# The last rows of a gated unit's weights: twelve rows a partition in the large load, eight small loads of equal rows on engines' own partitions

## The chip, the core and the metric

The kernel runs on one core of a Trainium2 chip. A core has engines with instruction streams of their own: PE (TensorE, matmuls), DVE (VectorE), ACT (ScalarE), POOL (GpSimd) and SP (SyncE, which here issues nearly all transfers). Sixteen DMA engines move data between HBM and SBUF, the on-chip memory of 128 partitions. The metric is the device time of one execution in microseconds (us), the median of several; here it was 199.22 us (three runs, 198.98 to 199.27). A change of less than about 0.2% can't be told from none.

## What is computed

One step of decoding for a batch of 8: a layer norm of x, attention over the last 2,048 entries of a key and value cache, and beside it a gated unit whose result scales the attention's output.

```python
W = min(4096, max(256, Sk // 4))                  # 2048
q = (xn @ wq).reshape(B, Sq, Hq, Dh)              # 8 x 1 x 32 x 128
scores = einsum("bhqd,bhkd->bhqk", q, k) * Dh ** -0.5   # k, v: the last W of the cache, 8 heads
o = einsum("bhqk,bhkd->bhqd", softmax(scores), v)
s = o.reshape(B, Sq, Hq * Dh) @ wo                # 4096 -> 512

g = einsum("bsd,df->bsf", xn, w_gate)             # D = 512, F = 1792
u = einsum("bsd,df->bsf", xn, w_up)
h = sigmoid(g) * u
d = einsum("bsf,fd->bsd", h, w_down)              # w_down: 1792 x 512
return x + s * silu(d)
```

All inputs are bf16. The change concerns w_down and the transposed h that is multiplied with it.

## The kernel before

The order of the work is written out by hand. All large inputs are loaded by SP on one queue, in the order in which the requests stand in the list `todo` (`want_rows`, `want_down`, `want_side`, `want_cache`): w_gate and w_up in two loads each, w_down, the two halves of wq, then 16 tiles of keys and 16 of values (2 MB each, 128 partitions x 16,384 bytes), the values three tiles behind, and wo in four pieces (16, 10, 4 and 2 of its 32 rows a partition). A tile needs one of nine slots (`empty`, L85); a request whose slot isn't free waits, and all behind it (`pump`, L87). SP also waits, for each load, for the one eight places earlier: there are eight completion semaphores for these loads.

A load over 128 partitions is spread evenly over the sixteen DMA engines, eight rows to each. A load over fewer partitions uses fewer engines.

The 1,792 rows of w_down are split. `want_down` (L143) loads the first 11 x 128 = 1,408 rows, 11 consecutive rows to a partition, so that a partition's piece is 11,264 bytes. The other 384 go into the tile `side` by eight small loads (`want_side`, L122; the list `sides`, L174):

- four of 15 rows a partition, over 5, 5, 3 and 3 partitions (`LOW`, `SF`): partitions q, q + 4, q + 8, ..., of the first 20, q being 0 to 3;
- four of 4 rows a partition, over 9 partitions each (`MID`, `SM`): partitions 32 + q, 32 + q + 4, and so on up to 67.

`side` must hold zeros where nothing is loaded in its first 32 partitions, so POOL clears them first (L126) and SP's first small load waits for that. Two small loads stand before the first half of wq in the queue, three before the second, three behind it.

PE multiplies xn with w_gate and w_up (L278, L294), ACT and DVE make h, and h is turned into columns: 11 transposes for the large part, 15 for the side part (L328), the latter from `h_side`, in which POOL has put the columns of h in the order of the side's partitions (L312, L320). DVE and ACT copy the result to `hT_sb` (L331, L333). Then 26 matmuls with 128, 68 or 20 rows make d (`d_ps`, L366), before the first transposes of keys (L456).

After that the loop over the batch runs: transposes of keys on PE with copies on DVE (L456, L461), scores (L474), softmax (L487 to L556), values (L584). It ends with the output projection `fin_ps` (L706), which takes wo's rows in the order in which they land, two operations on DVE (L717, L719) and the write of the output (L721).

Of the kernel before, what the change touches and what calls it, by code (L numbers as in the profile page):

```python
# [10 lines left out]
def kernel(  # L11
# [13 lines left out]
    nc = tc.nc  # L25
    P = 128
    B, _, D = A_x.shape
# [4 lines left out]
    F = B_w_gate.shape[1]  # L32
# [15 lines left out]
    bf16 = mybir.dt.bfloat16  # L48
# [12 lines left out]
    work = ctx.enter_context(tc.tile_pool(name="work", bufs=1))  # L61
# [20 lines left out]
    weights = {}  # L82
# [25 lines left out]

        todo.append((True, f))

    LOW, SF = (5, 5, 3, 3), 15
    MID, SM = 9, 4
    SP = 4 * max(LOW)
    M_AT = 32
    MP = 4 * MID
    MT = 11
    m0 = MT * P
    m1 = m0 + SF * sum(LOW)
    assert m1 + SM * MP == F
    side = {}  # L120

    def want_side(w, q, at, count, rows, base, of):  # L122
        def f(tag=None):
            if tag:
                t = slots.tile([P, SF, w.shape[1]], bf16, name="side", tag=tag)
                nc.gpsimd.memzero(t[:M_AT])  # L126
                side["t"] = t
                rows_of[("side", 0)] = (t, tag)
                for r in range(SF):
                    weights[("wd_sb", MT + r)] = t[: M_AT + MP if r < SM else SP, r]  # L130
            q0.dma_start(  # L131
                out=side["t"][at + q : at + q + 4 * (count - 1) + 1 : 4, :rows].rearrange(
                    "p s n -> p (s n)"
                ),
                in_=w[base : base + of * count * rows, :].rearrange(
                    "(p q s) n -> q p (s n)", q=of, s=rows
                )[q % of],
            )

        todo.append((not side, f))  # L140
        side["asked"] = True

    def want_down(w):  # L143
        def f(tag):
            t = slots.tile([P, MT, w.shape[1]], bf16, name="wd_sb", tag=tag)
            q0.dma_start(
                out=t[:].rearrange("p t n -> p (t n)"),
                in_=w[: MT * P, :].rearrange("(p t) n -> p (t n)", t=MT),
            )
            rows_of[("wd_sb", 0)] = (t, tag)  # L150
            for r in range(MT):
                weights[("wd_sb", r)] = t[:, r, :]

        todo.append((True, f))
# [16 lines left out]
    want_rows("wg_sb", B_w_gate, KT, 0, KT, 2)  # L171
    want_rows("wu_sb", B_w_up, KT, 0, KT, 2)
    want_down(B_w_down)
    sides = []  # L174
    for q in range(4):
        sides.append((q, 0, LOW[q], SF, m0 + q // 2 * 2 * LOW[0] * SF, 2))
        sides.append((q, M_AT, MID, SM, m1, 4))
    for x in sides[:2]:
        want_side(B_w_down, *x)
    for i in range(2):  # L180
        want_rows("wq_sb", A_wq, KT, 2 * i, 2 * i + 2)
        for x in sides[2 + 3 * i : 5 + 3 * i]:
            want_side(B_w_down, *x)
# [7 lines left out]
    for t0, t1 in ((0, 16), (16, 26), (26, 30), (30, RT)):  # L191
# [15 lines left out]
        out=perm[:].rearrange("k (l p) -> k l p", l=G),  # L207
        in_=ident[:].rearrange("k (p l) -> k l p", l=G),
# [11 lines left out]
        out=rstd[:], in_=mv[:, 1:2], func=AF.Sqrt, bias=eps_t[:], scale=1.0  # L220
# [4 lines left out]
        out=xn_bf[:],  # L225
# [8 lines left out]
    for kt in range(KT):  # L234
        nc.tensor.transpose(  # L235
            out=xnT_ps[:, kt, :],
            in_=xn_bf[:].rearrange("b (p kt) -> b kt p", kt=KT)[:, kt, :],
# [5 lines left out]

    hT_sb = work.tile([P, MT + SF, Z], bf16, name="hT_sb")
    nc.gpsimd.memzero(hT_sb[:])  # L245
    oP_sb = work.tile([P, RT, Z], bf16, name="oP_sb")
    nc.gpsimd.memzero(oP_sb[:])
    h_side = work.tile([B, SF, M_AT + MP], bf16, name="h_side")
    nc.gpsimd.memzero(h_side[:])

    NB = D // P
# [11 lines left out]
    with nc.allow_low_precision(reason="zeros and a one"):  # L263
        nc.vector.reduce_sum(
            out=band[:], in_=ident[:].rearrange("k (q t) -> k q t", t=RT), axis=AX.X
        )
        nc.vector.reduce_sum(
            out=pick[:], in_=ident[:].rearrange("k (q t) -> k t q", t=RT), axis=AX.X
# [21 lines left out]
    h_bf = ktpool.tile([P, CU * P], bf16, name="h_bf", tag="kT")  # L290
    for k in range(F // FC):
        u_ps = ps_t.tile([B, FC], f32, name="u_ps", tag="t")
        for kt in range(KT):
# [8 lines left out]
            out=h_bf[:B, k * FC : (k + 1) * FC],  # L302
# [5 lines left out]
    hT_ps = ps_m.tile([P, MT + SF, B], bf16, name="hT_ps", tag="m")  # L308
    for h in range(2):
        c = LOW[2 * h]  # L310
        at = m0 + h * 2 * LOW[0] * SF
        nc.gpsimd.tensor_copy(  # L312
            out=h_side[:, :, : 4 * c].rearrange("b t (e q) -> b t e q", q=4)[
                :, :, :, 2 * h : 2 * h + 2
            ],
            in_=h_bf[:B, at : at + 2 * c * SF].rearrange(
                "b (e q t) -> b t e q", q=2, t=SF
            ),
        )
    nc.gpsimd.tensor_copy(  # L320
        out=h_side[:, :SM, M_AT:],
        in_=h_bf[:B, m1:F].rearrange("b (p t) -> b t p", t=SM),
    )
    cuts = [h_bf[:B, :m0].rearrange("b (p t) -> b t p", t=MT)[:, t] for t in range(MT)]
    rows = [P] * MT + [M_AT + MP] * SM + [SP] * (SF - SM)
    cuts += [h_side[:, t, : rows[MT + t]] for t in range(SF)]
    for t, x in enumerate(cuts):
        nc.tensor.transpose(  # L328
            out=hT_ps[: rows[t], t, :], in_=x, identity=ident[:B, :B]
        )  # L330
    nc.vector.tensor_copy(out=hT_sb[:, :MT, :B], in_=hT_ps[:, :MT])  # L331
    for k, t0, t1 in ((M_AT + MP, MT, MT + SM), (SP, MT + SM, MT + SF)):
        nc.scalar.copy(out=hT_sb[:k, t0:t1, :B], in_=hT_ps[:k, t0:t1])  # L333

    def fold(out_ps, src, start, stop):
        for j in range(NB):
# [38 lines left out]
    for e in range(2):  # L375
# [3 lines left out]
        for r in range(rep):  # L379
            nc.tensor.transpose(  # L380
                out=qT_ps[:, r].rearrange("p g z -> p (g z)"),
                in_=q_bf[:, r * Dh : (r + 1) * Dh],
# [3 lines left out]
            out=qm_sb[:, :, G * e : G * (e + 1), M0 : M0 + rep].rearrange(  # L386
                "p b g r -> p r g b"
            ),
            in_=qT_ps[:, :, :, :B],
# [14 lines left out]
    for j in range(NB):  # L404
# [15 lines left out]
        out=turn_rows[:].rearrange("k (x l r) -> k x l r", x=NU, l=G),  # L420
        in_=ident[:].rearrange("k (l x r) -> k x l r", x=NU, l=G),
    )
    sel_e = consts.tile([P, 2, Hq], f32, name="sel_e")
    for e in range(2):
        nc.vector.reduce_sum(
            out=sel_e[:, e, :].rearrange("k (i h) -> k i h", i=NQ),
            in_=ident_f[:].rearrange(
                "k (i m e h) -> k e i h m", i=NQ, m=NJ // 2, e=2
            )[:, e],
# [290 lines left out]
    for j in range(NB):  # L720
        (q0, q1)[j % 2].dma_start(  # L721
            out=out.flatten_outer_dims()[:, j * P : (j + 1) * P],
            in_=y_bf[Z * j : Z * j + B, :],
# [31 lines left out]
```

## Time and profile before

| what | value |
|---|---|
| time, median of three runs | 199.22 us |
| the profiled execution: time, span of instructions | 199.33 us, 197.5 us |
| busy: PE, DVE, ACT, POOL | 80%, 63%, 21%, 6% of the span |
| moved by DMA | 81.32 MB in 6,396 packets, mean 412 GB/s |
| DMA, GB/s from 40 to 160 us | 429 |
| the issue of one small load on SP | 690 to 864 ns |
| POOL's clearing of `side`, 32 partitions x 3,840 words | 3,287 ns |

The trace also keeps a record of each DMA packet: one row of a load is one packet here. Durations in this execution:

```
bytes    packets   duration, ns
 2,048     128      84
 4,096     164     159
 7,168     512     272 in 465 cases, up to 1,412 in the first microsecond
10,240     128     385
11,264     128     422
15,360      16     573
16,384   4,480     611 in 4,437 cases, up to 1,159
16,384      16     879 to 962 (instructions, queue q8)
```

Share of busy time is an average; what matters for an edit is which wait ends last where it acts. In the profile's chain of waits, a DMA entry is the time from the issue of a load until the work that waited for it could start.

### The profile page before, as it was taken

To read this page: it belongs to the slowest core of one execution; us is meant where nothing else is said; L and a number is where in the kernel's file an instruction comes from. 1 tells how busy PE (TensorE), PEld (TensorE's weight loads), DVE (VectorE), ACT (ScalarE), POOL (GpSimd) and SP (SyncE) were. 2 spreads that over 40 slices of the span, in tenths; PEclk is the share of its full clock that TensorE was granted. 3 is DMA by queue.
4 is the path that set the end of the run, shared out by engine and by line. 5 is a ranking of instruction groups with operands and counts; after the bars stand their busy time and mean duration, and the time that the engine had idled before them with its cause. 6 is when DMAs were issued, how large, how long until landed. Compare 5 with 4: busy or idle time off the path is not lost.

```text
span 197.5 us, 4796 instructions
## 1 busy us (share of the span) xinstructions
PE 157.4 (80%) x2112; PEld 103.1 (52%) x2112; DVE 125.4 (63%) x245; ACT 40.7 (21%) x95; POOL 11.0 (6%) x22
## 2 busy tenths in 40 slices
PE   0089559999788898799979987999799979976733
PEld 0034325776664565466545654566466556655531
DVE  4623106999797696679666965796669658935201
ACT  0522022006306001600160016001600160071000
POOL 8910200000000000000000000000000000000000
PEclk9999859999999999999999999999999999999975
DMA  6999999999999999999999999999999999999980
GB/s 205 424 440 435 431 434 435 425 425 431 423 425 425 438 428 435 431 425 428 422 433 431 435 425 433 428 418 428 428 438 431 428 428 431 428 423 425 428 366 21
DMA packets 6396, 81.32 MB, mean 412 GB/s; under 512 B 812, under 2 KB 820, under 8 KB 1624
## 3 DMA queue, kind: packets, MB, share of 16 engines
q1 hardware_dynamic: 6328, 81.01, 96.6%
q8 instruction: 16, 0.26, 0.5%
q10 hardware_dynamic: 48, 0.01, 0.0%
q14 instruction: 4, 0.03, 0.0%
HBM read 81.01 MB, written 0.01 MB: 410 GB/s over the span
## 4 chain that ended last, share of the span: by engine, by line
DMA 73%; PE 22%; POOL 3%; SPq 0%; issue 0%; DVE 0%; POOLq 0%
DMA v_sb<-in_A_v_cache_dram 46%; DMA wo_sb<-in_A_wo_dram 14%; PE kT_ps L456 11%; DMA wq_sb<-in_A_wq_dram 7%; DMA k_sb<-in_A_k_cache_dram 6%; PE o_ps L584 4%; PE s_ps L474 3%; POOL side L126 2%; PE m_ps L614 1%; PE fin_ps L706 1%; PE pT_ps L563 1%; SPq L131 0%; POOL perm L206 0%; POOL hT_sb L245 0%; DVE prod L717 0%
## 5 line engine op out<-in xcount | busy, mean ns | idle before, releaser
L461 DVE COPY kT_sb<-kT_ps 128x1024 bf16<-128x1024 bf16 x128 | 84.2, 683 | 28.9 <-PE kT_ps L456 25.0
L456 PE MATMUL kT_ps<-perm,k_sb 128*128 128x128 bf16 x1024 | 72.6, 220 | 3.7 <-DMA k_sb<-in_A_k_cache_dram 3.7
L456 PEld LDWEIGHTS <-k_sb 128*128 128x128 bf16 x1024 | 58.8, 98 | 26.1 <-issue 16.8
L584 PE MATMUL o_ps<-v_sb,pT_sb 128*32 128x256 bf16 (+1 forms) x352 | 36.5, 327 | 9.0 <-DMA v_sb<-in_A_v_cache_dram 7.6
L474 PE MATMUL s_ps<-kT_sb,qm_sb 128*32 128x512 bf16 x256 | 25.6, 389 | 1.3 <-DVE kT_sb L461 1.1
L494 ACT ACTIVATE p_buf<-s_ps,st 32x512 bf16<-32x512 f32 x32 | 21.7, 679 | 15.4 <-DVE st L487 15.1
L584 PEld LDWEIGHTS <-pT_sb 128*32 128x32 bf16 (+1 forms) x352 | 12.3, 101 | 21.7 <-issue 19.7
L604 ACT ACTIVATE o_sb<-o_ps,fac 128x512 f32<-128x512 f32 (+1 forms) x8 | 4.9, 608 | 60.9 <-PE o_ps L584 60.9
L568 DVE COPY pT_sb<-pT_ps 128x1024 bf16<-128x1024 bf16 x16 | 10.8, 676 | 1.8 <-PE pT_ps L563 1.8
L474 PEld LDWEIGHTS <-qm_sb 128*32 128x32 bf16 x256 | 7.0, 93 | 8.0 <-issue 1.3
L563 PE MATMUL pT_ps<-turn_rows,p_buf 128*128 128x128 bf16 x128 | 10.7, 227 | 0.0
L563 PEld LDWEIGHTS <-p_buf 128*128 128x128 bf16 x128 | 9.4, 149 | 0.2 <-issue 0.2
L521 ACT ACTIVATE w_row<-w 1x128 f32<-1x128 f32 x8 | 2.5, 309 | 30.6 <-DVE w L514 30.6
L235 PE MATMUL xnT_ps<-ident,xn_bf 8*128 8x8 bf16 x4 | 0.3, 176 | 10.6 <-DVE xn_bf L224 10.6
L385 DVE COPY qm_sb<-qT_ps 128x128 bf16<-128x128 bf16 x2 | 1.4, 881 | 8.7 <-PE qT_ps L380 8.7
L301 DVE TENSOR_TENSOR h_bf<-sig,u_ps 8x448 bf16<-8x448 f32 x4 | 2.4, 608 | 6.6 <-PE u_ps L294 6.1
L278 PE MATMUL g_ps<-wg_sb,xnT_sb 128*8 128x448 bf16 x16 | 5.7, 544 | 0.3 <-DVE xnT_sb L242 0.3
L494 ACT ACTIVATION_READ_ACCUMULATOR p_buf<-s_ps,st 32x1 f32 x32 | 5.9, 184 | 0.0
L706 PE MATMUL fin_ps<-wo_sb,oP_sb 128*32 128x128 bf16 x128 | 3.3, 263 | 3.1 <-DMA wo_sb<-in_A_wo_dram 3.1
L487 DVE TENSOR_REDUCE st<-s_ps 128x1 f32<-128x512 f32 x8 | 5.4, 681 | 0.5 <-PE s_ps L474 0.5
L235 PEld LDWEIGHTS <-xn_bf 8*128 8x128 bf16 x4 | 0.2, 117 | 10.6 <-DVE xn_bf L224 10.6
L352 PE MATMUL q_ps<-wq_sb,xnT_sb 128*32 128x512 bf16 x32 | 3.1, 526 | 3.2 <-DMA wq_sb<-in_A_wq_dram 3.2
(88 smaller groups left out, 92.0 us busy)
## 6 DMA issues: line engine op xcount, KB each, us to landing
k_sb<-in_A_k_cache_dram SPq DMA_DIRECT2D x16, 2048.0 KB
v_sb<-in_A_v_cache_dram SPq DMA_DIRECT2D x16, 2048.0 KB
wq_sb<-in_A_wq_dram SPq DMA_DIRECT2D x2, 2048.0 KB
wo_sb<-in_A_wo_dram SPq DMA_DIRECT2D x1, 2048.0 KB
wg_sb<-in_B_w_gate_dram SPq DMA_DIRECT2D x2, 896.0 KB
wu_sb<-in_B_w_up_dram SPq DMA_DIRECT2D x2, 896.0 KB
wd_sb<-in_B_w_down_dram SPq DMA_DIRECT2D x1, 1408.0 KB
wo_sb<-in_A_wo_dram SPq DMA_DIRECT2D x1, 1280.0 KB
```

The lines of the kernel that those rows point to most:

```text
L126: nc.gpsimd.memzero(t[:M_AT])
L278: nc.tensor.matmul(g_ps[:], lhsT=xnT_sb[:, kt, :B], rhs=weights[("wg_sb", kt)][:, k * FC : (k + 1) * FC], start=(kt == 0), stop=(kt == KT ...
L456: nc.tensor.transpose(out=kT_ps[:, c, :], in_=k_sb[:, j * CU + h * CH + c, :], identity=perm[:],)
L461: nc.vector.tensor_copy(out=kT[(b, u)][:, h * CH : (h + 1) * CH, :], in_=kT_ps[:])
L474: nc.tensor.matmul(s_ps[b][NR * l : NR * (l + 1), :], lhsT=qm_sb[:, b, i * G + l, o : o + Z], rhs=t[:, :, PG * l : PG * (l + 1)], start=(u ...
L487: nc.vector.tensor_reduce(out=st[b][:], in_=s_ps[b][:], axis=AX.X, op=ALU.max, negate=True)
L494: nc.scalar.activation(out=p_buf[b % 2][rows, :, l, :], in_=s[rows, :].rearrange("k (c p) -> k p c", p=PG), func=AF.Exp, bias=st[b][rows, ...
L563: nc.tensor.transpose(out=pT_ps[:, c, :], in_=p_buf[b % 2][:, :, :, h * CH + c].rearrange("k p l -> k (p l)"), identity=turn_rows[:],)
L568: nc.vector.tensor_copy(out=pT[b][:, h * CH : (h + 1) * CH, :], in_=pT_ps[:])
L584: nc.tensor.matmul(o_ps[r] if b < WIDE else o_ps[r, 0:2], lhsT=pT[b][:, c, r], rhs=x, start=(c == 0), stop=(c == CU - 1), tile_position=(0 ...
L604: nc.scalar.activation(out=o[:, :n], in_=o_ps[:, :n], func=AF.Copy, scale=fac.pop(b)[:])
L706: nc.tensor.matmul(fin_ps[Z * j : Z * (j + 1), :], lhsT=oP_sb[:, t, :], rhs=weights[("wo_sb", t)][:, j * P : (j + 1) * P], start=(t == 0), ...
```

## The change

The large load takes 12 rows a partition (1,536 rows) instead of 11. The small loads bring the last 256 rows: 16 rows a partition, in two halves of 8 (8,192 bytes each), over 5, 5, 3 and 3 partitions. Their partitions lie 8 apart instead of 4 (`EP = P // 16`): a small load of pair h and parity q fills partitions p, p + 8, p + 16, ... with p = 2 (2h + q), that is 0, 2, 4 or 6. The loads over nine partitions are gone; the number of small loads, eight, and their places in the queue stay. POOL clears 40 partitions of `side` over 16 rows. `h_side` has 40 columns, of which every second stays zero; one of POOL's three copies and one of ACT's two go. There are 28 transposes and matmuls for d, 12 with 128 rows and 16 with 40.

```diff
-    LOW, SF = (5, 5, 3, 3), 15
-    MID, SM = 9, 4
-    SP = 4 * max(LOW)
-    M_AT = 32
-    MP = 4 * MID
-    MT = 11
+    LOW, SF = (5, 5, 3, 3), 16
+    EP = P // 16
+    SP = EP * max(LOW)
+    MT = 12
     m0 = MT * P
-    m1 = m0 + SF * sum(LOW)
-    assert m1 + SM * MP == F
+    assert m0 + SF * sum(LOW) == F

-    def want_side(w, q, at, count, rows, base, of):
+    def want_side(w, h, q, a, z):
         def f(tag=None):
             if tag:
                 t = slots.tile([P, SF, w.shape[1]], bf16, name="side", tag=tag)
-                nc.gpsimd.memzero(t[:M_AT])
+                nc.gpsimd.memzero(t[:SP])
...
+            n = LOW[2 * h]
+            at = m0 + 2 * h * LOW[0] * SF
+            p = 2 * (2 * h + q)
             q0.dma_start(
-                out=side["t"][at + q : at + q + 4 * (count - 1) + 1 : 4, :rows].rearrange(
-                    "p s n -> p (s n)"
-                ),
-                in_=w[base : base + of * count * rows, :].rearrange(
-                    "(p q s) n -> q p (s n)", q=of, s=rows
-                )[q % of],
+                out=side["t"][p : p + EP * (n - 1) + 1 : EP, a:z],
+                in_=w[at : at + 2 * n * SF, :].rearrange(
+                    "(p q s) n -> q p s n", q=2, s=SF
+                )[q, :, a:z],
             )
...
-    for q in range(4):
-        sides.append((q, 0, LOW[q], SF, m0 + q // 2 * 2 * LOW[0] * SF, 2))
-        sides.append((q, M_AT, MID, SM, m1, 4))
+    sides = [
+        (h, q, a, a + SF // 2)
+        for h in range(2)
+        for q in range(2)
+        for a in (0, SF // 2)
+    ]
...
-    nc.gpsimd.tensor_copy(
-        out=h_side[:, :SM, M_AT:],
-        in_=h_bf[:B, m1:F].rearrange("b (p t) -> b t p", t=SM),
-    )
...
-    rows = [P] * MT + [M_AT + MP] * SM + [SP] * (SF - SM)
-    cuts += [h_side[:, t, : rows[MT + t]] for t in range(SF)]
+    cuts += [h_side[:, t] for t in range(SF)]
+    rows = [P] * MT + [SP] * SF
...
-    for k, t0, t1 in ((M_AT + MP, MT, MT + SM), (SP, MT + SM, MT + SF)):
-        nc.scalar.copy(out=hT_sb[:k, t0:t1, :B], in_=hT_ps[:k, t0:t1])
+    nc.scalar.copy(out=hT_sb[:SP, MT:, :B], in_=hT_ps[:SP, MT:])
```

## The prediction, made before the change was run

> **What bounds the kernel now.** I read the page's slices first, then its queues, the chain of waits, SyncE's own timeline, and last the trace's record of every DMA packet (start, duration, bytes, queue).
>
> ```profile
> DMA  6999999999999999999999999999999999999980
> GB/s 205 424 440 435 431 434 435 425 425 431 423 425 425 438 428 435 431 425 428 422 433 431 435 425 433 428 418 428 428 438 431 428 428 431 428 423 425 428 366 21
> q1 hardware_dynamic: 6328, 81.01, 96.6%
> q8 instruction: 16, 0.26, 0.5%
> ```
>
> From the second slice to the last but two the sixteen DMA engines are never below nine tenths. The kernel moves 81 MB and is as long as that takes. PE, busiest of the others, is at 80%.
>
> ```profile
> 1.84 3.23 POOL side L126
> ...
> 6.81 13.68 DMA wq_sb<-in_A_wq_dram
> ...
> 163.50 28.32 DMA wo_sb<-in_A_wo_dram
> 191.86 1.86 PE fin_ps L706 x52
> 193.74 0.43 PE fin_ps L706 x8
> 194.19 0.30 DVE prod L717
> ```
>
> The chain (start, length, what) ends with the output weights landing: PE starts its last 8 matmuls at 193.74, when the last load is in, and the rest is fixed work (197.5 of span, 199.33 of time; that execution lies 0.11 above the median of 199.22). So the question is when the last engine has finished its last packet.
>
> ```profile
> 5.09 1.68 SPq L131 DMA_DIRECT2D side<-in_B_w_down_dram  x2
> 6.81 0.46 SPq L101 DMA_DIRECT2D wq_sb<-in_A_wq_dram  x1
> ...
> 20.51 2.58 SPq L159 DMA_DIRECT2D k_sb<-in_A_k_cache_dram  x4
> ...
> 57.01 0.53 SPq L159 DMA_DIRECT2D v_sb<-in_A_v_cache_dram  x1
> ```
>
> SyncE (first column the start) issues far ahead. The load issued at 57.01 is the thirteenth cache load; twelve such loads before it occupy even the quickest engine until 83. The cover is 26 us there and, worked out in the same way for the other loads, never under 14 from 26.73 on, so no engine runs dry.
>
> The packet records say who is last. On one engine packets follow each other end to start (4 ns overlap), so each engine's stream can be followed through its completion writes. A 16,384-byte packet takes 611 ns in 4,437 of 4,480 cases, 607 from start to start: 27 GB/s, sixteen times that is 432. The engines differ only in two things: the small side loads and the instruction packets. Row k of a small load goes to engine k: three streams hold four packets of 15,360 bytes, two hold two, four more hold only the 4,096s, seven none. Each 16,384-byte instruction packet (queue q8) delays the stream of its engine by some 1.42 us; they go round two of engines 5-8 and six of 9-15, twice. Two streams with equal phase were told apart by that order. Four smaller ones (q14) cost engines 0-4 another 0.55 to 0.85 each. Last completion, in us of the span (packet clock less 11.34):
>
> ```
> engines   small loads now          last completion
> 0-2       4 x 15360 + 4 x 4096     192.86  192.90  193.45
> 3-4       2 x 15360 + 4 x 4096     192.10  193.27
> 5-8       4 x 4096                 190.34  190.96  192.12  193.60
> 9-15      none                     189.99  192.86  192.92  193.02  193.14  193.18  193.25
> ```
>
> The last is one of 5-8 with two instruction packets: 193.60, and PE's 193.74 follows.
>
> **The change by bytes.** Same 81 MB, same 51 loads.
> - Large load L146: 12,288 bytes a row for 11,264. Between 422 ns (11,264) and 611 (16,384) lies 460: 8 rows x 38 ns = +0.30 us on every engine.
> - Small loads: 8,192 bytes lie at 310 ns between 272 (7,168) and 385 (10,240). Engines 0-2 had 4 x 573 + 4 x 159 = 2.93 us and get 8 x 310 = 2.48: -0.45, net -0.15. Engines 3-4: 1.78 to 1.24, net -0.24. Engines 5-8 lose 4 x 159 and four completion writes, -0.64, net -0.34. Engines 9-15 net +0.30.
> - The end by this: 193.60 - 0.34 = 193.26 on the old last engine, 193.25 + 0.30 = 193.55 on the new one. Sum -0.05 us.
>
> **Edits costed at nothing.** POOL's memset L126 (3.29 us for 3,840 words a row) gets 4,096: +0.22, and SyncE's first L131, wq_sb and all behind move with it. The chain counts this memset, but its cover is the queue: wg, wu and wd keep the engines busy to 14.6, while wq_sb is issued at 6.81. Without cover it would cost 0.22. The other memsets are +0.03 and -0.19. One of three POOL copies (L320, 0.30) and one of two ACT copies (L333) go; two transposes and two d_ps matmuls (some 0.11 each at L366) come. These lie before the first kT at 32.49, behind those 14 us of cover; without it they cost about 0.2. The chain of eight loads in flight keeps its numbering: k_sb still waits for the first wq_sb.
>
> **The change by place.** A small load's rows now lie 8 partitions apart (row k at 8k + 0, 2, 4 or 6) instead of 4 (4k + q, and 32 + 4k + q). Do these writes cross another engine's? In the large loads no engine ever stretches another, and the old small packets, 573 ns sixteen times and 159 each time, neither were stretched nor stretched a neighbour. Had engine k owned partitions 8k to 8k+7, nearly all old small packets would have crossed (engine 1's to 4-7, the 4,096s at 32-63). So either crossing costs nothing or the groups are 4 partitions wide with a second set 32 further on, which the old places fit for all nine engines. In that second case the new places cross: engine 1 writes to 8-11 (engine 2's) and 12-15 (3's), 2 to 16-19 (4's) and 20-23 (5's), 3 to 24-27 (6's), 4 to 32-35 (0's), 0 at last to 4-7 (1's).
>
> The trace of before holds no crossing, so its price is bounded. Low: nothing; the six 1,024-byte packets of x_bf overlapped in partitions 0-7 at 44 ns each, though so little may be held in buffers. High: an instruction packet of 16,384 bytes, which shares an engine instead, costs its stream 1.42 us, 8,192 bytes by that 0.71. Between, if two streams halve one path: 0.303 to each per packet. I take 0.303, the fair share; the fetch also has a latency that data in a queue doesn't.
>
> Each of engines 0-4 crosses or shares with four packets at the least: +1.21. On 0-2, that gives 193.45 - 0.15 + 1.21 = 194.51 for the latest, +0.91. Engine 3 crosses with four and is hit by four of engine 1's: +2.42, so 192.10 - 0.24 + 2.42 = 194.28, or, if it is the other of its pair, 195.45 (+1.85). If only the one that is hit loses, the end is +0.6 to +0.9. I take +1.1: 199.22 + 1.1 = 200.3 (the profiled execution 200.4). At 0.71 for four packets: 193.45 - 0.15 + 2.84 = 196.14, +2.5, 201.8.
>
> The Trainium skill speaks against this change in the same place. SBUF — State Buffer, section "Door 1: The DMA port swizzle", says that four neighbouring partitions and the four 32 further on share one write port of 27.2 GB/s, not eight neighbours. DMA: Bandwidth & Descriptors, section "The descriptor swizzle", gives one engine to one port in 128-row loads, on this chip's hardware queues too. By these, the old places are each engine's own and the new ones are not, and two streams on one port halve: an estimate of 8,192 / 27.2 = 0.30 us a packet, the same sum. The unstretched packets of before agree with it; no run so far shows a crossing.
>
> **Rivals.**
> - *Crossing is free (0.27).* Then only bytes count: 199.22 - 0.05 = 199.17, not slower. For it: x_bf's overlapping packets, and the small loads are only 256 KB, some of which may wait in buffers. Against: sixteen engines keep 432 GB/s only in loads where the rows fit the groups. It decides if engines 0-3 end by 193.6.
> - *Eight neighbours are one engine's own, as the change has it, and something was lost before (0.08).* The old last engine then shows its full -0.34: 198.88. Against: 9-15 get +0.30 whatever else happens and stood at 193.25, so it needs start phases that favour them by 0.3 (the engines' ends of wd spread from 14.56 to 15.28 here).
> - *Crossing at the fetch's price, or engines 1 and 2 hit as often as they hit (0.15, within the slower side).* Price +2.5: 201.8. Against: while one engine writes elsewhere its own path is free, so the five small loads partly pass each other.
> - *The rest, 0.50, is the forecast*, +0.6 to +1.85.
>
> **How the numbers follow.** The likeliest is 200.3, its own range 199.8 to 201.1. The first rival lies at 199.17 with a spread of 0.15 between executions, so the range reaches from 199.0 to 201.6: it leaves out half of the 0.08 and more than half of the 0.15. About 0.2% (0.4 us) is what a measurement can tell from no change. Slower by more: 0.50 + 0.15, less 0.04 for a small price within 0.4 us, 0.61. Within: 0.27 + 0.04, and part of the second rival, 0.32. Faster by more: 0.07.
>
> **What would show it.** Right: small packets of 8,192 bytes above 310 ns (up to 600), 16,384-byte packets near 900 to 1,200 in the stretch from 14 to 32 us on engines 3, 5 and 6 besides those beside instruction packets, GB/s in that stretch below 430, and the last completion on one of engines 0-4. Wrong: 8,192 bytes at 310 ns throughout and the last completion on one of 9-15 near 193.55. The sum by bytes fails if 12,288 bytes take other than 460 ns, or if an engine idles between loads.

## The result and the profile after

The changed kernel takes 201.05 us (median of four, 200.86 to 201.41) against 199.20: 1.0098 times as long, interval 1.0083 to 1.0113. It is slower, by 1.85 us. Its profiled execution has a span of 199.5 us (197.5 before) and a time of 201.41 (199.33).

The slices of the changed kernel's page, and its queues:

```profile
DMA  6999999999999999999999999999999999999980
GB/s 214 420 447 406 373 340 437 427 437 424 419 440 427 427 420 437 434 434 420 427 434 422 443 420 430 432 424 437 417 430 434 430 437 417 424 435 430 423 354 19
q1 hardware_dynamic: 6288, 81.01, 96.6%
q8 instruction: 16, 0.26, 0.5%
```

The same megabytes pass through engines that count as just as busy. But in the fourth, fifth and sixth slice (a slice is 5 us; these reach from 15 to 30 us) they move 406, 373 and 340 GB/s, where the kernel before moved 435, 431 and 434. An engine whose packet takes longer is as busy as before, so the DMA digits show nothing; the row of GB/s shows it. These slices are where the small loads run.

The end of its chain of waits (start, length, what):

```profile
165.36 28.52 DMA wo_sb<-in_A_wo_dram
193.88 0.04 issue
193.92 1.26 PE fin_ps L702 x30
...
195.82 0.43 PE fin_ps L702 x8
...
196.27 0.30 DVE prod L713
```

The same last steps as before, 2.08 us later (prod at 196.27 for 194.19). Nothing was lost behind the loads.

SP's timeline in the changed kernel:

```profile
5.31 1.62 SPq L131 DMA_DIRECT2D side<-in_B_w_down_dram  x2
6.98 0.43 SPq L101 DMA_DIRECT2D wq_sb<-in_A_wq_dram  x1
...
21.56 2.58 SPq L157 DMA_DIRECT2D k_sb<-in_A_k_cache_dram  x4
...
59.53 0.54 SPq L157 DMA_DIRECT2D v_sb<-in_A_v_cache_dram  x1
```

The first small load is issued 0.22 later, as the longer memset has it, and this vanishes: wq_sb follows 0.17 later than before and the engines are still busy with w_down then. The keys are issued 1.05 later, because they wait for the first half of wq, which lands later; they are still issued before the second half of wq has been moved.

The packet records show where the time went. (The packet clock's offset to the span differs from execution to execution; from here on it is taken from each profile's own first instruction, which lies at 0.24.) The durations in the changed kernel:

```
12,288 bytes   128 packets    460 ns in 126 cases
 8,192 bytes    32 packets    309 ns in 14 cases, 18 longer, up to 642
16,384 bytes    in three stretches at the small loads (14 to 32 us) 92 longer than 620,
                up to 1,313; elsewhere only beside instruction packets
```

The lengthening in the three stretches, summed and divided by the sixteen engines, is 0.31, 0.71 and 0.90 us: 1.93 for an engine on the mean. It isn't the loss of a few of them: the streams that can be followed from end to end lost 1.86 to 1.91, and one that holds no small load goes 611, 908, 616 in the first stretch, 825, 1,033, 685 in the second and 1,086, 1,029 in the third.

### The profile page after: what moved, and what is told of

Its sections match the earlier page's. It is cut to its first block, busy times and chain, and to the rows that moved or that the text cites. A ratio compares the mean times of both kernels' runs of the same rounds, so it can differ in the third digit from the quotient of the medians.

```text
span 199.5 us, 4801 instructions
## 1 busy us (share of the span) xinstructions
PE 162.1 (81%) x2116; PEld 105.4 (53%) x2116; DVE 125.7 (63%) x245; ACT 40.7 (20%) x94; POOL 10.9 (5%) x21
## 4 chain that ended last, share of the span: by engine, by line
DMA 72%; PE 25%; SPq 1%; DVE 0%; issue 0%
DMA v_sb<-in_A_v_cache_dram 45%; DMA wo_sb<-in_A_wo_dram 14%; PE kT_ps L452 11%; DMA wq_sb<-in_A_wq_dram 8%; DMA wu_sb<-in_B_w_up_dram 5%; PE o_ps L580 4%; PE s_ps L470 3%; PE d_ps L362 2%; PE m_ps L610 1%; PE fin_ps L702 1%; PE pT_ps L559 1%; PE q_ps L348 1%; SPq L101 1%; PE qT_ps L376 0%; PE b_ps L333 0%
## 5 line engine op out<-in xcount | busy, mean ns | idle before, releaser
L452 PE MATMUL kT_ps<-perm,k_sb 128*128 128x128 bf16 x1024 | 73.9, 222 | 3.0 <-DMA k_sb<-in_A_k_cache_dram 3.0
L452 PEld LDWEIGHTS <-k_sb 128*128 128x128 bf16 x1024 | 60.1, 99 | 25.6 <-issue 18.3
L580 PE MATMUL o_ps<-v_sb,pT_sb 128*32 128x256 bf16 (+1 forms) x352 | 38.6, 342 | 7.7 <-DMA v_sb<-in_A_v_cache_dram 6.9
L580 PEld LDWEIGHTS <-pT_sb 128*32 128x32 bf16 (+1 forms) x352 | 13.1, 106 | 21.3 <-issue 18.4
L279 PE MATMUL g_ps<-wg_sb,xnT_sb 128*8 128x448 bf16 x16 | 5.2, 507 | 0.3 <-DVE xnT_sb L242 0.3
L610 PE MATMUL m_ps<-ident_f,o_sb 128*128 128x32 f32 x40 | 5.3, 276 | 0.0
```

The costliest lines, as they stand in the source:

```text
L279: nc.tensor.matmul(g_ps[:], lhsT=xnT_sb[:, kt, :B], rhs=weights[("wg_sb", kt)][:, k * FC : (k + 1) * FC], start=(kt == 0), stop=(kt == KT ...
L452: nc.tensor.transpose(out=kT_ps[:, c, :], in_=k_sb[:, j * CU + h * CH + c, :], identity=perm[:],)
L580: nc.tensor.matmul(o_ps[r] if b < WIDE else o_ps[r, 0:2], lhsT=pT[b][:, c, r], rhs=x, start=(c == 0), stop=(c == CU - 1), tile_position=(0 ...
L610: nc.tensor.matmul(oT_ps, lhsT=o[:, e, :], rhs=sel[:, e], start=(e == 0), stop=(e == n - 1),)
```

## The experiments

Twelve kernels were run, each beside the kernel before on the same chip. "Loss" below is the lengthening of packets of 25 to 42 us of the packet clock (the three stretches), divided by sixteen. In the code, `...` stands for lines left out; in every run the places in `h_side` follow those in `side`. The windows that are shown give, for a stretch of the span: its length, busy time and number of instructions of PE, PE's weight loads, DVE, ACT and POOL, the granted clock of PE, the DMA share, and GB/s last. First the kernel before, then the changed one:

```profile
14.00:20.00 6.00, 5.82 (x25) 2.27 (x23) 1.90 (x4) 1.60 (x3) 0.00 (x0) 1.00 1.01 433
20.00:25.00 5.00, 2.59 (x42) 1.66 (x43) 0.74 (x2) 0.30 (x2) 1.22 (x4) 0.80 1.00 428
25.00:30.00 5.00, 3.29 (x31) 1.23 (x30) 0.00 (x0) 1.08 (x2) 0.00 (x0) 0.52 1.02 434
```

```profile
14.00:20.00 6.00, 5.42 (x25) 2.16 (x23) 2.30 (x4) 1.60 (x3) 0.00 (x0) 1.00 1.01 411
20.00:25.00 5.00, 2.81 (x44) 1.74 (x45) 0.34 (x2) 0.26 (x1) 1.02 (x3) 0.71 1.01 369
25.00:30.00 5.00, 2.16 (x24) 0.92 (x27) 0.00 (x0) 0.58 (x2) 0.00 (x0) 0.50 0.98 342
```

**Places alone (e1).** The changed kernel with the small rows 4 partitions apart again.

```diff
-    EP = P // 16
+    EP = 4
...
-            p = 2 * (2 * h + q)
+            p = 2 * h + q
...
```

> The changed kernel with its small loads' rows 4 partitions apart again (row k at 4k + 2h + q), everything else as changed: same sources, sizes, number of loads. Theory A (the writes cross: each engine has a group of four partitions and a second 32 further on, and the changed places leave it): no stretched packets in the stretch of the small loads, 16,384 bytes at 611 ns there, and a time near 199.15, the sum by bytes (-0.05 against before). Theory B (the reads do it: rows 32 KB apart in HBM, a power of two, against 30 KB before): still slow, about 201.0, packets of all engines stretched as in the changed kernel.

Measured: 199.18, ratio 1.0002 (0.9993 to 1.0012). Its windows:

```profile
14.00:20.00 6.00, 5.23 (x26) 2.18 (x25) 2.44 (x4) 1.60 (x3) 0.00 (x0) 1.00 1.03 442
20.00:25.00 5.00, 2.81 (x44) 1.71 (x45) 0.21 (x1) 0.25 (x1) 1.01 (x3) 0.68 0.99 421
25.00:30.00 5.00, 3.34 (x32) 1.20 (x35) 0.00 (x0) 1.09 (x2) 0.00 (x0) 0.50 1.02 434
```

The dip is gone, all 32 small packets take 309 ns, and of the large ones in 25 to 42 us one is longer by 36 ns and two by 7. The whole loss lies in the places. What is left of the change, its bytes, is worth nothing that can be measured.

**One group further (e2), and the kernel before moved (e3).** In e2 the rows of e1 stand four partitions higher; in e3 those of the four 15-row loads of the kernel before do.

```diff
 e2, against e1
-            p = 2 * h + q
+            p = EP + 2 * h + q
...
 e3, against the kernel before
-        sides.append((q, 0, LOW[q], SF, m0 + q // 2 * 2 * LOW[0] * SF, 2))
+        sides.append((q, 4, LOW[q], SF, m0 + q // 2 * 2 * LOW[0] * SF, 2))
...
```

> As the run before with every small row four partitions further on (row k at 4(k + 1) + 2h + q), so that each of engines 0 to 4 writes to the next engine's group; sources and sizes unchanged. Theory A: slow again, 200 to 202, packets stretched in the small loads' stretch. Theory B: the same time as with the rows unshifted, whatever that is. If eight neighbouring partitions belonged to one engine, half of the rows would cross in either kernel and both would be alike.

> The kernel before with the rows of its four 15-row loads four partitions further on (4(k + 1) + q), nothing else. Theory A: 16 packets of 15,360 bytes now cross; slow, 200 to 202, with stretched packets that the kernel before doesn't have. Theory B: 199.2 as before, since the reads are unchanged.

Measured: e2 200.06, ratio 1.0052 (1.0037 to 1.0067); e3 200.36, 1.0064 (1.0049 to 1.0079). Both are slow as theory A has it. A step of four partitions, with nothing else changed, makes the kernel before slower by 0.6%; of its sixteen 15,360-byte packets, all at 573 ns before, six are longer now. In e2 the five rows of a load move to five neighbouring groups, so that while all five engines are in their small loads only the last meets a large load: in the first stretch the loss is 0.04, and two 16,384-byte packets carry nearly all of it.

**The source (e4).** The changed kernel, its small loads reading rows 30 KB apart (of w_down, partly other rows than the 256 that are meant).

```diff
-            at = m0 + 2 * h * LOW[0] * SF
+            at = m0 + 2 * h * LOW[0] * 15
...
-                in_=w[at : at + 2 * n * SF, :].rearrange(
-                    "(p q s) n -> q p s n", q=2, s=SF
-                )[q, :, a:z],
+                in_=w[at : at + 2 * n * 15, :].rearrange(
+                    "(p q s) n -> q p s n", q=2, s=15
+                )[q, :, a - a // 8 : z - a // 8],
```

> The changed kernel with its places in SBUF, but the small loads read rows 30 KB apart in HBM instead of 32 KB (and, with that, partly other rows of w_down: the gated unit's last rows are not the right ones). Sizes and numbers of packets are the same. Theory A: as slow as the changed kernel, about 201.0. Theory B: about 199.15, no stretched packets.

Measured: 201.20, ratio 1.0109 (1.0093 to 1.0126), and the dip is there:

```profile
14.00:20.00 6.00, 5.65 (x25) 2.23 (x23) 2.07 (x4) 1.60 (x3) 0.00 (x0) 1.00 1.01 408
20.00:25.00 5.00, 2.59 (x44) 1.68 (x45) 0.57 (x2) 0.26 (x1) 1.02 (x3) 0.76 1.02 375
25.00:30.00 5.00, 2.08 (x20) 0.85 (x23) 0.00 (x0) 0.50 (x2) 0.00 (x0) 0.50 1.01 359
```

Theory B, the pitch of the reads, falls.

**32 and 64 further (e5, e6).** Rows at 32 + 4k + 2h + q, and at 64 + 4k + 2h + q.

```diff
-            p = 2 * h + q
+            p = OFF + 2 * h + q        # OFF = 32; 64
...
```

> The changed kernel with small rows at 32 + 4k + 2h + q. Theory A says that the group of four 32 partitions further on belongs to the same engine: 199.2, no stretched packets. If it belonged to another, about 200.1 as with the rows shifted by four.

> The changed kernel with small rows at 64 + 4k + 2h + q, which by theory A are the groups of engines 8 to 12; no two small loads then share a group, every packet meets another engine's large load. Theory A1 (only the two engines that meet lose, 0.30 us each per packet): engines 0-2 and 8-10 lose 2.4 us, 8-10 hold two instruction packets each and end near 195.6 of the span, time about 201.5, while the engine without side loads and instruction packets keeps 611 ns throughout. Theory A2 (a contested group slows all sixteen, as all sixteen lost some 1.9 us in the changed kernel): all streams are stretched alike, time 200.5 to 201.5.

Measured: e5 199.17, ratio 1.0004 (0.9995 to 1.0014), in the stretches of the small loads no packet is longer. e6 201.89, 1.0137 (1.0120 to 1.0154). The second set, 32 further, is the engine's own; the one 64 further belongs to others. Of e6's theories A1 falls: every engine is stretched, by 2.9 us on the mean. Some 0.6 of that is of a kind that only this run shows: after the first two loads every stream runs seven packets or so at 700 ns, with no small load in flight.

```profile
14.00:20.00 6.00, 5.23 (x27) 2.22 (x26) 2.43 (x4) 1.60 (x3) 0.00 (x0) 1.00 1.02 371
20.00:25.00 5.00, 3.70 (x44) 2.37 (x45) 0.21 (x1) 0.26 (x1) 1.02 (x3) 0.63 1.02 342
25.00:30.00 5.00, 1.28 (x16) 0.54 (x19) 0.00 (x0) 0.00 (x0) 0.00 (x0) 0.50 1.03 362
```

**Consecutive partitions (e7).**

```diff
-    EP = P // 16
+    EP = 1
...
-            p = 2 * (2 * h + q)
+            p = 2 * h * LOW[0] + q * n
...
```

> The changed kernel with the small rows on consecutive partitions (0-4, 5-9, 10-12, 13-15), the plainest placement: up to four engines then write into one group at once. Theory A, with the group as the limit: the first load puts 4 x 8,192 bytes into one group, 1.2 us instead of 0.3, and the same for the others, so slower than the changed kernel, 202 to 204. If a crossing cost a fixed amount whatever it meets, about 201.

Measured: 202.88, ratio 1.0188 (1.0173 to 1.0204). The plainest placement is the dearest: a loss of 3.4 us a stream on the mean, single packets of 16,384 bytes up to 1,677 ns over their 611. It depends on what is met, not on the crossing as such.

**Three, one and two crossing engines (e9, e10, e12).** The five-row loads stay in their own groups; of the three-row loads, all three, one or two rows leave theirs. These were run last, to see when engines that take no part begin to lose.

```diff
-            p = 2 * (2 * h + q)
+            p, e = (66 + q, EP) if h else (q, EP)    # e9; e10: (2 + q, 36); e12: (2 + q, 60)
...
-                out=side["t"][p : p + EP * (n - 1) + 1 : EP, a:z],
+                out=side["t"][p : p + e * (n - 1) + 1 : e, a:z],
...
```

> The step-4 kernel with only the four three-row loads at 66 + 4k + q, the five-row loads in their own groups: 12 packets cross instead of 32, in four loads instead of eight. All 32 cost 2.7 us (at 64). If the cost goes with the packets: +1.0, 200.2; if it goes with the loads, that is with the time in which any group is contested: +1.35, 200.55. Engines that take no part are stretched as well in both.

> As the run before, but the three rows lie at 2 + q + 36k, so that engines 0 and 1 stay in their own groups and only engine 2 crosses (into 72 to 75): 4 packets in four loads. By packets: an engine that takes no part loses 0.3 in all; by time contested: 1.35, as with three. If only the two engines that meet lose (theory A1): none on the others, 1.2 on two engines, and the time +1.1 at most, less if these are not the last. By the first and the last the time is 199.2 to 200.3.

> Between one and three: the three-row loads at 2 + q + 60k, so that engine 0 stays in its group and engines 1 and 2 write to 62-63 (by theory A engine 7's) and 122-123 (engine 14's). One crossing engine left all the others at 611 ns; three at once stretched every engine by 0.95 us in the last stretch of three loads. If the stall of all needs three crossing engines: the others at 611 ns, time +0.9 as with one. If it begins with two: the others lose 0.2 to 0.6 in that stretch.

Measured: e9 200.30, 1.0049 (1.0034 to 1.0064); e10 200.17, 1.0042 (1.0027 to 1.0057); e12 200.11, 1.0049 (1.0032 to 1.0065). The windows that hold the last three of the three-row loads, for e9, e10 and e12:

```profile
25.00:30.00 5.00, 3.27 (x32) 1.43 (x35) 0.00 (x0) 1.08 (x2) 0.00 (x0) 0.50 1.02 352
```

```profile
25.00:30.00 5.00, 2.88 (x28) 1.24 (x31) 0.00 (x0) 1.09 (x2) 0.00 (x0) 0.50 0.99 415
```

```profile
25.00:30.00 5.00, 3.45 (x40) 1.54 (x43) 0.00 (x0) 1.09 (x2) 0.00 (x0) 0.55 1.00 352
```

The times are alike, the ways are not. With one crossing engine the others' packets in that stretch stay at 611. Only the two engines that meet lose: two small packets (+0.03, +0.31) and three large ones (1,107, 928, 1,068 for 611), 1.61 us together for three crossing packets, or 0.54 a packet for both, near the 2 x 0.303 of the fair share (0.22 of it on the crossing stream, 0.32 on the one that is hit). The time is +0.86 because the last stream is now one with two instruction packets that lost about 1 us here, by its completions the one that was hit. (Four other large packets, near 24.5 us, were longer by 0.74 together; I have no reason for them. Near the same place single packets are longer without any crossing too, but less: 635 ns before, 647 in e1, 631 and 676 in e11.) With two crossing engines every stream loses in that stretch, 0.86 on the mean, with three 0.98: the step lies between one and two, and a third adds little. And it takes more than one load: in the stretch before, where a single three-row load crosses, e12 loses 0.01 and e9 0.06. Neither "by packets" nor "by time" describes this; e10 agrees with A1, and e9 and e12 with A2. That the number of crossing engines makes the step is the plainest reading, but not separated from whom they meet: by theory A e10 writes into engine 10's group, e12 into those of 7 and 14, and each kernel was profiled once.

**A balanced kernel (e8, e11).** The streams' ends before lay between 189.99 and 193.60, so rows were moved to engines that ended early: four loads of 12 rows over seven engines and one of 16 rows over three, all in own groups; e11 cuts three of these in two.

```diff
 e8, against the kernel before
-    LOW, SF = (5, 5, 3, 3), 15
-    MID, SM = 9, 4
+    SE, SR, SF = 7, 12, 16
...
+                    out=side["t"][q : q + 4 * (SE - 1) + 1 : 4, :SR].rearrange(
+                        "p s n -> p (s n)"
+                    ),
...
+                    out=side["t"][32:SP:4].rearrange("p s n -> p (s n)"),
 e11, against e8: three of the four loads of 12 rows are cut into two of 6
```

> A kernel for the gap that the engines' ends show: the large load of 11 rows a partition as before, four small loads of 12 rows over seven engines (4k + q) and one of 16 rows over three (32 + 4k), all in the engines' own groups, five loads instead of eight. By the sum: engines 5 and 6 +1.2, 7 and 8 -0.64, 0-2 -0.5, 9-15 as before, which then end last at 193.25 instead of 193.60: -0.35, time 198.85, 0.9982 of before (198.6 to 199.2).

> The balanced kernel with three of its small loads cut in two, eight small loads again, same rows, engines and partitions; SP has 48 instructions instead of 46. Theory: 1.0 us of the balanced kernel's loss came from an 8 KB instruction packet that fell at 196.8, between the two output writes on SP, because SP's stream was shorter; with 48 the packet falls near 176 again, the output takes 2.7 instead of 3.7 us, and the time is 200.3. Rival: the output was slow for another reason and stays so, 201.3. The rest, +1.1, comes from engines that carry two instruction packets and a small load, and stays.

Measured: e8 201.31, ratio 1.0118 (1.0101 to 1.0134), a miss; e11 200.24, 1.0048 (1.0031 to 1.0064). In e8 no packet of the small loads' stretches is longer, in e11 three, by 65 ns at most, so the places are right. Two other things went wrong. The two of engines 5 to 8 that hold instruction packets are among the seven (in e8 two streams with small loads of 12 rows show two instruction packets each), so that they got rows instead of being relieved: the last completion is at 194.67, 1.07 later than before. And the output became slower, by SP's timeline in e8 and in e11:

```profile
195.81 1.09 SPq L711 DMA_DIRECT2D out_dram<-y_bf  x2
```

```profile
196.34 0.68 SPq L714 DMA_DIRECT2D out_dram<-y_bf  x2
```

In e8 the packet records have an 8,192-byte instruction packet at 197.48, and the last packet of SP's second output write follows it, at 197.99 (the others of that write lie at 197.6 to 197.7); before and in e11 the last packet of that kind falls at 176.2 and 179.0. The span ends 3.7 us after the output's issue in e8, 2.7 in e11. By the traces SP issues 50 transfers in e8, and 53 in e11 as in the kernel before; the 46 and 48 of the expectation stand in no trace. So with e11 the theory holds for the output, and the rival falls. That this packet holds SP's instructions is inferred from its time and from SP's slow issue (1.09 us for 0.68); no view names whose instructions a packet holds. No kernel here beats the one before.

## Why the prediction was right, and where it was not

- *The bound.* Right. All of it is DMA: the chain's last steps moved as a whole, and a loss before 32 us reached the end undiminished (1.93 a stream, 2.08 at the chain's end in the profiled execution, 1.85 between the medians).
- *The sum by bytes, -0.05.* Right: e1 has the changed bytes in own places, ratio 1.0002. 12,288 bytes take the 460 ns that were read off, 8,192 take 309 for 310. Its last completion is at 193.44 of its own span (193.55 was worked out), on a stream without small loads.
- *Edits at nothing.* Right as far as e1 goes, which holds them all: the memset's 0.22 is seen at SP's first small load and nowhere later.
- *Groups of four with a second set 32 further.* Right, and shown from several sides: own groups (e1, e5) without stretched packets, other groups (e2, e3, e6) slow. The argument from the unstretched 573 ns of the kernel before was enough to choose between the readings. What the Trainium skill's SBUF — State Buffer, section "Door 1: The DMA port swizzle", says of the partitions of a port agrees in all of these.
- *The price, 0.303 to each of the two.* About right for one crossing engine: e10, 0.54 a packet for both together against 0.61, from three packets of one execution.
- *Who loses.* This is the step that failed. "Each of engines 0-4 crosses or shares with four packets at the least: +1.21" left engines 9 to 15 with their +0.30 only, and the end to one of 0-4. In the changed kernel all sixteen lost some 1.9, and in e12 and e9 all sixteen lost as soon as two or three engines crossed for more than a packet or so. The long 16,384-byte packets, expected on engines 3, 5 and 6, came on every engine, and the last stream was one without any small load, with two instruction packets, at 195.68. So +1.1 came out as +1.85. The median still lies inside the likeliest's own range (199.8 to 201.1), and +1.85 is even what was worked out for an unlucky engine 3; that is luck, since the sum reached it by delaying other engines than the chip did.
- *The rivals.* "Crossing is free" falls with e1 against e2. "Eight neighbours are one engine's own" falls too: e3 would then be no worse than the kernel before.

What holds up streams that write where no one else writes is not shown. No view says what a packet waits for. The Trainium skill's DMA: Bandwidth & Descriptors, section "Back-pressure in remote DMA", says of transfers between cores that a full SBUF port holds back the engines on its path, those sharing the path too; that would fit, but no run here shows such a path, or tests whether the reads or the writes stand still.

## What to carry to other kernels

In a kernel that keeps all sixteen DMA engines busy, look at where a small load's rows land, not only at how many bytes each engine gets: row k of a load over a few partitions goes to engine k, and it is free at 4k to 4k + 3 or 32 further on (seen for k up to 6; the kernel before had k = 7 at 60 to 63, also without a longer packet). For k = 8 only 64 to 67 was seen to be free, in the kernel before; 32 to 35 are engine 0's by e5. Elsewhere it is dear, by 0.4 to 1.9% in these runs. Take GB/s per slice against the same slices of the kernel before; the busy digits can't show a stretched packet. Before rows are moved to an engine for balance, find out in the packet records which engines also fetch instructions, about 1.42 us for each 16 KB.

## What the runs showed that was not expected

- One crossing engine costs the two that meet; two cost all sixteen, 0.86 us each in one stretch of three loads; three 0.98 (one profile of each).
- With three transfers fewer on SP (e8), the last 8 KB instruction packet moved from 176 to 197.5 us, among the writes of the output, and the output took 3.7 us instead of 2.7.
- Moving four small loads by four partitions (e3) makes a kernel of 81 MB slower by 0.64%, though these loads carry 0.25 MB.
